# Gated linear attention with a gelu feed-forward: loads and weights no longer wait for each other, w_in in four pieces, and a new order of the instructions

## The chip, the core and the metric

The kernel runs on one core of a Trainium2 chip. The metric is the device time of one execution in microseconds (us), lower is better; the time before is the median of three runs. The core has five engines, each with a queue of its own that it works through in order: PE (matmuls; PEld is its weight load), DVE (vector), ACT (activation functions), POOL (GpSimd) and SP, which here only issues DMA transfers. POOL issues DMA transfers too. All transfers share 16 DMA engines.

## The reference

q, k, v and f_logit have the shape (4, 8, 768, 48): batch, heads, sequence, head dimension. Each head runs a gated linear recurrence over the sequence, and the result goes through a feed-forward layer with exact gelu.

```python
f = 1.0 / (1.0 + np.exp(-f_logit))
for t in range(S):
    state = f[:, :, t, :, None] * state + np.einsum('bhd,bhe->bhde', k[:, :, t], v[:, :, t])
    y[:, :, t] = np.einsum('bhd,bhde->bhe', q[:, :, t], state)
x = y.transpose(0, 2, 1, 3).reshape(B * S, H * D)     # 3072 x 384
h = x @ w_in                                          # 384 x 2048
g = 0.5 * h * (1.0 + erf(h * inv_sqrt2))
out = g @ w_out                                       # 2048 x 384
```

## The kernel before

The 3072 rows are 24 chunks of 128, numbered 0 to 23; two chunks make one of twelve units, numbered 0 to 11 (so "the second unit" is unit 1, "the third unit" unit 2). A unit is also one group of the feed-forward layer.

For each unit, f_logit, k, q and v (384 KB each) are loaded: names in the load list are a letter and the unit, so f0, k0, q0, v0. w_in comes in column pieces i0, i1, ..., w_out in four pieces o0 to o3; both are issued by POOL, and the data loads by SP.

The steps of a unit u with chunks n = 2u, 2u+1 are:

- E, L on ACT: exp and log of the gates. C on PE: their running sums (the C of unit 2 is C4). RG, GT, GL on ACT: exps of the sums. G on DVE: the second chunk's sum as a difference.
- KP, QP on DVE or POOL: k and q times these exps. VC on POOL or ACT: v cast to bf16.
- Tk, Tq on PE: transposes of both; KQ on DVE or ACT copies them out of PSUM. From unit 4 on a DMA transpose does this (KD).
- A on PE: scores. AM on DVE: mask. S on PE: state sum of a chunk pair. R on DVE, T and SB on POOL: the running state, and its cast to bf16.
- YI and YX on PE (or Y): output inside the pair, and from the state. YB on DVE or ACT: copy out. XT on PE and X on DVE or ACT: transposed into xT (later by a DMA transpose, XD).
- F1 on PE: eight steps of six matmuls for a group, each into one PSUM bank; GE on ACT: gelu of that bank, into gT. F2 on PE: for each chunk four steps of four matmuls; O copies out, and a store follows.

Step u of F1 reads w_in's columns 256u to 256u + 255, so with 1024 columns in the first piece steps 0 to 3 need i0 alone.

exp and log need another activation table than gelu. Wherever ACT goes from one to the other, a table load stands in its queue (ACT_TABLE_LOAD).

What sets the order is a list written out by hand: every step is added to a plan (`Plan.add`) with an engine and an assumed duration, and `ORDER` gives the sequence in which `Plan.run` places them. The placing gives each step a time from the assumed durations, waits and transfer times, and the instructions of each engine are then emitted by these times. The durations in the code thus decide order alone. While PE would idle in the first 30 us of the plan, it is given matmuls on a `junk` tile.

`load` adds the transfers in the sequence of `LOADS`. Where the sequence goes from SP's loads to POOL's weights or back, it looks backwards for a transfer of the other kind and makes the new one wait until that one has landed (`gate`).

Of the kernel before, what the change touches and what calls it, by code (L numbers as in the profile page):

```python
# [11 lines left out]
ALU = mybir.AluOpType  # L12
# [9 lines left out]
TURN = 0.1  # L22
# [53 lines left out]
class Plan:  # L76
# [30 lines left out]
    def run(self):  # L107
# [16 lines left out]
        while ready:  # L124
# [69 lines left out]
WIN = [1024, 512, 512]  # L194
# [8 lines left out]
HX = [0, 3, 9]  # L203
# [16 lines left out]
AHEAD = 4.4  # L220
UNITS = 12
WARM = 30.0
LOADS = ['f0', 'f1', 'k0', 'q0', 'v0', 'q1', 'k1', 'i0', 'v1', 'f2', 'q2', 'v2', 'k2', 'i1', 'i2', 'o0', 'o1', 'o3', 'o2', 'f3', 'f4', 'k3', 'q3', 'v4', 'v3', 'q4', 'k4', 'k5', 'f5', 'v5', 'q5', 'f6', 'v6', 'k6', 'q7', 'q6', 'f7', 'k7', 'v7', 'f8', 'k8', 'v8', 'q8', 'u9', 'u10', 'u11']
# [38 lines left out]
def kernel(  # L262
# [143 lines left out]

    def load(eng, issue, wr, bufs, dur, name):
        i = len(order)
        gate = None
        if i and eng != "act" and order[i - 1][0] != eng:  # L410
            ahead = 0.0
            late = None
            for j in range(i - 1, -1, -1):
# [3 lines left out]
                if order[j][0] != eng:  # L417
                    late = order[j][1]
# [285 lines left out]
    def compact(n):  # L704
        return rc[n] // nC in DENSE
# [576 lines left out]
```

## Time and profile before

| what | value |
|---|---|
| median of 3 runs (lowest, highest) | 179.34 us (178.78, 179.63) |
| profiled execution, first to last instruction | 178.1 us |
| PE busy | 168.7 us |
| ACT busy | 130.0 us |
| ACT table loads | 1 ahead of the first exp, and 17 |
| filler matmuls on PE (junk) | 26 |
| granted PE clock | 1.0 throughout |

The profiled execution is given on the page by its span, from its first instruction to its last. Rows of the timeline have start, duration, engine, line, operation, output and inputs, how many instructions are merged, and in brackets how long the engine was idle before and what ended that. Rows of stretches give the stretch and its length, then busy time and instruction count of PE, PEld, DVE, ACT and POOL, then the clock, the DMA share and GB/s. Rows of the chain have start, duration and what the time is put down to; SPq is SP's queue. Matmuls overlap by their fill and drain, so the chain's rows, which count from start to start, are better for adding up.

### The profile page before, as it was taken

The page shows a single profiled execution, that of the slowest core. Times are in us where ns is not written, and L with a number is a line of the kernel's source. Part 1 is how long each engine was busy: PE and PEld are TensorE (multiplying, and loading weights), DVE is VectorE, ACT ScalarE, POOL GpSimd, SP SyncE. Part 2 cuts the span into 40 slices and gives each one's busy share as a digit, 9 for nine tenths or more (in the row PEclk, how much of TensorE's full clock was granted, in tenths as well). Part 3 has the DMA queues.
Part 4 walks back from the last instruction along what each step waited for, and adds up shares of the span by engine and source line. Part 5 has one row for each costly group of instructions (what it writes and reads, how often), then busy time and mean ns, then how long its engine had stood idle before and what let it go on. Part 6 is the DMA issues. An engine that isn't in the chain of part 4 may idle for free.

```text
span 178.1 us, 4916 instructions
## 1 busy us (share of the span) xinstructions
PE 168.7 (95%) x1996; PEld 131.2 (74%) x1996; DVE 93.7 (53%) x188; ACT 130.0 (73%) x221; POOL 55.2 (31%) x119
## 2 busy tenths in 40 slices
PE   7787889999997999999999999999999999999993
PEld 2345679866787787886688689866797976887972
DVE  5188750067988556338677681246582276560110
ACT  2954399967797999989477597786684789951630
POOL 7267595041126801501052334002222504410000
PEclk9999999999999999999999999999999999999999
DMA  5999999999979898988999999999899975405412
GB/s 140 261 261 214 277 179 195 213 221 256 235 154 227 187 212 188 202 178 169 233 174 248 188 174 204 188 220 156 191 238 179 232 165 81 85 4 112 138 60 88
DMA packets 106997, 32.61 MB, mean 183 GB/s; under 512 B 102112, under 2 KB 106080, under 8 KB 106976
## 3 DMA queue, kind: packets, MB, share of 16 engines
q1 hardware_dynamic: 105056, 29.07, 79.0%
q0 software_dynamic: 1776, 3.15, 10.0%
q8 instruction: 15, 0.25, 0.6%
q10 hardware_dynamic: 144, 0.10, 0.2%
q14 instruction: 6, 0.05, 0.1%
HBM read 25.17 MB, written 4.72 MB: 168 GB/s over the span
## 4 chain that ended last, share of the span: by engine, by line
PE 72%; DMA 14%; SPq 6%; POOL 3%; issue 1%; DVE 1%; ACT 0%; DVEq 0%; POOLq 0%
PE ps L1165 30%; PE ps L1186 29%; DMA vt<-in_v_dram 6%; SPq L513 4%; DMA kt<-in_k_dram 4%; DMA kq<-sc 3%; PE ps L995 2%; PE ps L1031 2%; PE ps L1211 1%; DMA out_dram<-osb 1%; PE ps L585 1%; PE ps L969 1%; SPq L949 1%; SPq L1200 1%; POOL vb L647 1%
## 5 line engine op out<-in xcount | busy, mean ns | idle before, releaser
L1175 ACT ACTIVATE gT<-ps 128x512 bf16<-128x512 f32 x96 | 57.2, 665 | 18.4 <-PE ps L1165 17.6
L1165 PE MATMUL ps<-xT,win 128*128 128x256 bf16 x576 | 69.0, 273 | 0.8 <-DMA win<-in_moe_w_in_dram 0.7
L1186 PE MATMUL ps<-wout,gT 128*128 128x384 bf16 x368 | 67.0, 326 | 0.0
L1165 PEld LDWEIGHTS <-win 128*128 128x128 bf16 x576 | 61.7, 114 | 3.7 <-DMA win<-in_moe_w_in_dram 0.9
L1186 PEld LDWEIGHTS <-gT 128*128 128x128 bf16 x368 | 34.1, 98 | 18.7
L901 DVE TENSOR_TENSOR am<-ps,mask 128x512 bf16<-128x512 f32 x28 | 17.5, 683 | 18.5 <-PE ps L995 18.5
L1248 ACT ACT_TABLE_LOAD x17 | 21.8, 1283 | 0.3
L640 DVE TENSOR_TENSOR sc<-kt,rg 128x384 bf16<-128x384 f32 x19 | 11.5, 606 | 15.8 <-ACT rg L607 11.1
L1191 DVE COPY osb<-ps 128x384 f32<-128x384 f32 x20 | 10.7, 552 | 16.8 <-PE ps L1186 15.7
L927 POOL TENSOR_TENSOR tn<-rr,gl 128x384 f32<-128x384 f32 x12 | 10.7, 889 | 25.1 <-DVE rr L925 19.1
L647 POOL CAST vb<-vt 128x384 bf16<-128x384 f32 x18 | 9.5, 539 | 26.8 <-DMA vt<-in_v_dram 26.6
L901 DVE TENSOR_TENSOR am<-ps,maskp 128x512 bf16<-128x512 f32 x20 | 12.7, 683 | 5.3 <-PE ps L1061 3.8
L945 DVE CAST yb<-ps 128x384 bf16<-128x384 f32 x21 | 11.4, 555 | 7.6 <-PE ps L1031 5.6
L640 DVE TENSOR_TENSOR sc<-qt,gt 128x384 bf16<-128x384 f32 x20 | 13.3, 684 | 3.4 <-ACT gt L613 2.7
L558 ACT ACTIVATE fl<-fl 128x768 f32<-128x768 f32 x12 | 10.1, 842 | 5.0 <-DMA fl<-in_f_logit_dram 5.0
L932 POOL CAST sb<-tn 48x192 bf16<-48x192 f32 x30 | 10.7, 362 | 8.3 <-DVE tn L921 7.1
L613 ACT ACTIVATE gt<-ps 128x384 f32<-128x384 f32 x21 | 10.3, 495 | 3.8 <-PE ps L587 2.9
L607 ACT ACTIVATE rg<-ps 128x384 f32<-128x384 f32 x21 | 10.1, 494 | 3.5 <-PE ps L587 2.9
L640 POOL TENSOR_TENSOR sc<-kt,rg 128x384 bf16<-128x384 f32 x5 | 5.3, 1065 | 22.5 <-ACT rg L607 14.3
L561 ACT ACTIVATE lf<-fl 128x768 bf16<-128x768 f32 x12 | 10.2, 849 | 0.3
L925 DVE TENSOR_TENSOR rr<-ps,tn 128x384 f32<-128x384 f32 x12 | 6.7, 555 | 5.9 <-PE ps L1018 4.8
L1241 PE MATMUL ps<-junk 128*128 128x512 bf16 (+3 forms) x26 | 8.3, 448 | 1.3 <-POOL junk L1233 1.3
(85 smaller groups left out, 145.1 us busy)
## 6 DMA issues: line engine op xcount, KB each, us to landing
out_dram<-osb SPq DMA_DIRECT2D x19, 192.0 KB, 2.8
kt<-in_k_dram SPq DMA_DIRECT2D x14, 192.0 KB, 4.5
fl<-in_f_logit_dram SPq DMA_DIRECT2D x14, 192.0 KB, 3.9
vt<-in_v_dram SPq DMA_DIRECT2D x14, 192.0 KB, 3.9
qt<-in_q_dram SPq DMA_DIRECT2D x14, 192.0 KB, 3.7
fl<-in_f_logit_dram SPq DMA_DIRECT2D x5, 384.0 KB, 4.9
kt<-in_k_dram SPq DMA_DIRECT2D x5, 384.0 KB, 6.2
qt<-in_q_dram SPq DMA_DIRECT2D x5, 384.0 KB, 6.3
```

The lines of the kernel that those rows point to most:

```text
L613: P.add("ACT", 0.40, lambda g=gps[j], gtv=gtv: nc.scalar.activation(gtv(), g.t()[:, 0:HD].rearrange("q (p h d) -> q p h d", h=2, d=D), AF. ...
L640: P.add("POOL" if pl else "DVE", 0.80 if pl else 0.475, lambda a=a, y=y, j=j, w=w, pl=pl, b=(gtv if w else rg): (nc.gpsimd if pl else nc.v ...
L647: P.add("ACT" if hv else "POOL", 0.40 if hv else 0.47, lambda y=y, j=j, hv=hv: (nc.scalar.copy if hv else nc.gpsimd.tensor_copy)(y["vb"].t ...
L901: P.add("POOL" if pl else "DVE", 1.15 if pl else 0.61, lambda hh=hh, pl=pl: (nc.gpsimd if pl else nc.vector).tensor_tensor(ams[hh].t(), ap ...
L927: P.add("POOL", 0.83, lambda: nc.gpsimd.tensor_tensor(tn.t(), rr.t(), glb(), ALU.mult), rd=[("rr", n), ("gl", n)], wr=[("tn", n)], bufs=[r ...
L932: P.add("POOL", 0.36, lambda hh=hh: nc.gpsimd.tensor_copy(sb.t()[64 * hh:64 * hh + D, :, D * hh:D * hh + D], tn.t()[64 * hh:64 * hh + D, : ...
L945: P.add("ACT" if help_ else "DVE", 0.40 if help_ else 0.475, lambda: copier(help_)(yb.t()[:, i, :], yp.t()[:, 0:HD]), rd=[("yp", n)], wr=[ ...
L1165: nc.tensor.matmul(hps.t()[:, i * tok:(i + 1) * tok].rearrange("a (s t) -> a s t", s=s), col(fo)[:, kk, :], xT.t()[:, :, kk, :], start=(kk ...
L1175: nc.scalar.activation(to, fr, AF.Gelu)
L1186: nc.tensor.matmul(op.t()[:, 0:d_model], gT.t()[:, fo, s_ * C:(s_ + 1) * C], wout[fo // 4][:, fo % 4, :], start=(fo == 0), stop=(fo == FO ...
L1191: P.add("DVE" if od else "ACT", 0.475 if od else 0.40, lambda op=op, osb=osb, od=od: copier(not od)(osb.t(), op.t()[:, 0:d_model]), rd=[(" ...
L1248: nc.scalar.preload_act_table_set({"exp": "natural_log_exp_and_others", "gelu": "gelu_and_others"}[o.table])
```

## The change

The loads of SP wait for no weights any more, and the weights wait for loads at two points: i0 until unit 0's values (vt0) have landed, o1 until unit 2's keys (kt2) have. v1 goes ahead of w_in in the load list. w_in comes in four pieces of 512 columns in place of one of 1024 and two of 512. The second chunk's copies change engines: VC2 goes from POOL to ACT, T2 and the first half of SB2 from POOL to DVE, X3 from ACT to DVE. All assumed durations are changed, and with them the order.

```diff
-WIN = [1024, 512, 512]
+WIN = [512, 512, 512, 512]
-HX = [0, 3, 9]
+HX = [0, 9]
-AHEAD = 4.4
+VCE = {2: 'ACT'}
+FM = []
+TE = {2: 'DVE'}
+SBE = {(2, 0): 'DVE'}
+SBD = {"POOL": 0.38, "DVE": 0.22, "ACT": 0.27}
+GATE = {'i0': 'vt0', 'o1': 'kt2'}
-LOADS = ['f0', 'f1', 'k0', 'q0', 'v0', 'q1', 'k1', 'i0', 'v1', 'f2', 'q2', 'v2', 'k2', 'i1', 'i2', 'o0', 'o1', 'o3', 'o2', 'f3', ...]
+LOADS = ['f0', 'f1', 'k0', 'q0', 'v0', 'q1', 'k1', 'v1', 'i0', 'i1', 'i2', 'i3', 'f2', 'o0', 'k2', 'q2', 'v2', 'o1', 'o3', 'o2', 'f3', ...]
...
-                d += TABLE
+                t = max(t, free["ACT"] + TABLE)
...
     def load(eng, issue, wr, bufs, dur, name):
         i = len(order)
-        gate = None
-        if i and eng != "act" and order[i - 1][0] != eng:
-            ahead = 0.0
-            late = None
-            for j in range(i - 1, -1, -1):
-                if order[j][0] != eng and ahead >= (AHEAD if eng == "pool" else 1.4):
-                    gate = late if late is not None and ahead > 5.3 and eng == "pool" else order[j][1]
-                    break
-                if order[j][0] != eng:
-                    late = order[j][1]
-                ahead += order[j][1].dur
+        gate = dict((nm, x) for _, x, nm in order).get(GATE.get(name))
...
+    def copy_on(eng):
+        return {"ACT": nc.scalar.copy, "POOL": nc.gpsimd.tensor_copy, "DVE": nc.vector.tensor_copy}[eng]
...
-            hv = u in HVC
+            hv = VCE.get(n, "ACT" if u in HVC else "POOL")
...
-            P.add("POOL", 0.45, lambda: nc.gpsimd.tensor_tensor(small(tn), small(rr), glb(), ALU.mult),
+            e = TE.get(n, "POOL")
+            P.add(e, 0.29 if e == "DVE" else 0.54, lambda e=e: (nc.vector if e == "DVE" else nc.gpsimd).tensor_tensor(small(tn), small(rr), glb(), ALU.mult),
```

The order list itself is replaced. What it does is shown at three places, each before and after; tile numbers differ by one or two between the programs.

POOL at the start, before: win is w_in's piece, vb a cast of v, sc the products KP and QP of unit 1, sb the state cast SB0 that YX1 reads.

```order
L525 DMA win_70<-in_moe_w_in_dram 128x3x1024 [waits DMAHW3_49]
L647 CAST vb_103<-vt_85 128x384 [waits DMAHW4_49]
L647 CAST vb_104<-vt_85 128x384
L640 TENSOR_TENSOR sc_97<-qt_82,gt_115 128x8x48 [waits DMAHW5_49,Activation_49]
L640 TENSOR_TENSOR sc_98<-qt_82,gt_114 128x8x48 [waits Activation_49]
L640 TENSOR_TENSOR sc_97<-kt_78,rg_118 128x8x48 [waits DMAHW6_49]
L726 CAST sb_148<-tn_141 48x4x48 [waits DVE_49,Pool_49]
```

The first weight transfer is issued when unit 0's q has landed, and no other stands ahead of the state cast. The same place after the change:

```order
L519 DMA win_70<-in_moe_w_in_dram 128x3x512 [waits DMAHW4_49]
L644 CAST vb_104<-vt_86 128x384
L644 CAST vb_105<-vt_86 128x384
L637 TENSOR_TENSOR sc_98<-qt_83,gt_116 128x8x48 [waits DMAHW5_49,Activation_49]
L519 DMA win_71<-in_moe_w_in_dram 128x3x512
L637 TENSOR_TENSOR sc_98<-kt_79,rg_119 128x8x48 [waits DMAHW6_49]
L637 TENSOR_TENSOR sc_99<-qt_83,gt_114 128x8x48 [waits Activation_49]
L519 DMA win_72<-in_moe_w_in_dram 128x3x512
L724 CAST sb_149<-tn_142 48x4x48 [waits DVE_49]
L724 CAST sb_149<-tn_142 48x4x48 [waits Pool_49]
L644 CAST vb_107<-vt_87 128x384 [waits DMAHW7_49,Pool_49]
L519 DMA win_73<-in_moe_w_in_dram 128x3x512
```

The first piece waits for unit 0's v, the second and third are issued between the products, ahead of the state cast, and the fourth behind it and a cast of unit 1's v.

ACT behind the first copy into xT, before: fl and lf are E2 and L2 of unit 2, gT a gelu.

```order
L964 COPY xT_163<-ps_174 128x384
L558 ACTIVATE fl_91<-fl_91 128x768
L561 ACTIVATE lf_94<-fl_91 128x16x48
L1248 ACT_TABLE_LOAD
L1175 ACTIVATE gT_167<-ps_174 128x4x2x64
```

The exp and log of unit 2 stand ahead of the first gelu. After the change ACT has the table load and fourteen gelus behind the copy, and the last of these are followed by:

```order
L1177 ACTIVATE gT_169<-ps_174 128x4x2x64
L1177 ACTIVATE gT_169<-ps_172 128x4x2x64
L1250 ACT_TABLE_LOAD
L555 ACTIVATE fl_92<-fl_92 128x768
L558 ACTIVATE lf_95<-fl_92 128x16x48
L604 ACTIVATE rg_117<-ps_177 128x384
```

E2 and L2 have moved behind fourteen of the sixteen gelus of the first two groups, with a table load of their own.

SP from the last loads of unit 2 on, before: fl_89 and fl_90 are the gates of units 3 and 4, and DMASW is the semaphore of a weight transfer.

```order
L513 DMA vt_87<-in_v_dram 128x8x96 [waits DMAHW2_49]
L513 DMA kt_79<-in_k_dram 128x8x96 [waits DMAHW3_49]
L513 DMA fl_89<-in_f_logit_dram 128x8x96 [waits DMAHW4_49,DMASW5_49,Activation_49]
L513 DMA fl_90<-in_f_logit_dram 128x8x96 [waits DMAHW5_49,Activation_49]
```

The gates of unit 3 wait for a piece of w_out. The same place after the change:

```order
L507 DMA qt_84<-in_q_dram 128x8x96 [waits DMAHW2_49]
L507 DMA vt_88<-in_v_dram 128x8x96 [waits DMAHW3_49]
L507 DMA fl_90<-in_f_logit_dram 128x8x96 [waits DMAHW4_49,Activation_49]
L507 DMA fl_91<-in_f_logit_dram 128x8x96 [waits DMAHW5_49,Activation_49]
```

The wait for the weights is gone, and unit 2's keys now come ahead of its q and v.

More of the change, by code (lines that the diff above doesn't have):

```diff
@@ L429, in load @@
         prev = order[-1][1] if order else None
-        if prev is not None and eng != "act" and order[-1][0] != eng:
-            prev.lat = 2.2
         gd = [gate] if gate is not None else []
@@ L449, in load @@
             o.fn = lambda o=o: fn(o)
-        if 7 <= i and o.lat < 1.8:
-            o.lat = 2.0 if name == "i0" else 1.8 if i < 30 else 1.7
-        order.append((eng, o))
+        if eng != "act":
+            o.lat = LANDS.get(name, 1.36 if i < 7 else 1.55 if i < 13 else 1.65 if i < 22 else 2.5 if i < 27 else 3.3 if i < 45 else 2.4)
+        order.append((eng, o, name))
     def src(a, n):
@@ L645, in decays @@
                     port=True, name=f"{nm.upper()}{n}")
-            hv = u in HVC
-            P.add("ACT" if hv else "POOL", 0.40 if hv else 0.47, lambda y=y, j=j, hv=hv: (nc.scalar.copy if hv else nc.gpsimd.tensor_copy)(
+            hv = VCE.get(n, "ACT" if u in HVC else "POOL")
+            P.add(hv, {"ACT": 0.40, "POOL": 0.47, "DVE": 0.3}[hv], lambda y=y, j=j, hv=hv: copy_on(hv)(
                 y["vb"].t().rearrange("p (h d) -> p h d", h=H), half(u, x["vt"], j)),
@@ L725, in carry_hs @@
             for hh, r in enumerate(rows):
-                P.add("POOL", 0.30, lambda hh=hh, r=r: nc.gpsimd.tensor_copy(sb.t()[r, :, D * hh:D * hh + D], small(tn)[r]),
+                e = SBE.get((n, hh), "POOL")
+                P.add(e, SBD[e], lambda hh=hh, r=r, e=e: copy_on(e)(sb.t()[r, :, D * hh:D * hh + D], small(tn)[r]),
                       rd=[("tn", n)] + z_sb, wr=[("sb", n, hh)], bufs=[tn, sb], prio=pr + 2, name=f"SB{n}")
@@ L900, in mask_scores @@
                 continue
-            P.add("POOL" if pl else "DVE", 1.15 if pl else 0.61, lambda hh=hh, pl=pl: (nc.gpsimd if pl else nc.vector).tensor_tensor(
+            P.add("POOL" if pl else "DVE", 1.15 if pl else 0.605, lambda hh=hh, pl=pl: (nc.gpsimd if pl else nc.vector).tensor_tensor(
                 ams[hh].t(), aps[hh].t().rearrange("p (h t) -> p h t", t=C),
@@ L931, in carry @@
         for hh in range(2):
-            P.add("POOL", 0.36, lambda hh=hh: nc.gpsimd.tensor_copy(
+            P.add("POOL", 0.38, lambda hh=hh: nc.gpsimd.tensor_copy(
                 sb.t()[64 * hh:64 * hh + D, :, D * hh:D * hh + D],
@@ L1065, in attn_pair @@
                 if jk:
-                    P.add("PE", 0.70, lambda: [b[1]() for b in both], mode=1, rd=[("kq", n) for n in ns],
+                    P.add("PE", 0.485, lambda: [b[1]() for b in both], mode=1, rd=[("kq", n) for n in ns],
                           wr=[("ap", u, 0), ("ap", u, 1)], bufs=[kq] + sum([b[2] + b[3] for b in both], []),
@@ L1175, in gelu @@
                 nc.scalar.activation(to, fr, AF.Gelu)
-            P.add("ACT", 0.60 if perm(ns[0]) and ns[0] // 2 not in RST else 0.50, gelu, rd=[("h", g, u)], wr=[("gT", g, u)], bufs=[hps, gT], table="gelu", prio=pr - 1000,
+            P.add("ACT", 0.585 if perm(ns[0]) and ns[0] // 2 not in RST else 0.49, gelu, rd=[("h", g, u)], wr=[("gT", g, u)], bufs=[hps, gT], table="gelu", prio=pr - 1000,
                   name=f"GE{'q' * (s == 4)}{g}.{u}")
```

46 lines of the change are left out of this document (25 added, 21 removed), and 62 rows, old and new, of the table ORDER.

## The prediction

> **What bounds the kernel now.** I read the page's totals first, then busy time by stretch, then the chain that ended last, then the start engine by engine.
>
> ```profile
> span 178.1 us, 4916 instructions
> PE 168.7 (95%) x1996; PEld 131.2 (74%) x1996; DVE 93.7 (53%) x188; ACT 130.0 (73%) x221; POOL 55.2 (31%) x119
> ```
>
> PE (the matmuls) is busy for 95% of the span. The stretches say where the rest is:
>
> ```profile
> 0.00:19.30 19.30, 14.48 (x216) 7.96 (x216) 11.54 (x40) 10.74 (x19) 10.76 (x33) 1.00 1.08 226
> 19.30:25.00 5.70, 5.20 (x110) 4.12 (x111) 3.78 (x8) 3.78 (x5) 5.03 (x11) 1.00 1.14 233
> 24.92:173.00 148.08, 146.99 (x1651) 117.40 (x1649) 77.89 (x140) 115.26 (x197) 39.52 (x76) 1.00 0.89 179
> ```
>
> From 24.92 on PE is idle for only 148.08 - 146.99 = 1.09 us. Its work is the same after the change, so it can gain in two ways only: reach the unbroken part sooner, and lose those 1.09 us. Nearly all of them are one wait:
>
> ```profile
> 54.35 0.52 PE L1093 MATMUL ps<-vb,sc 64*128 64x96 bf16 x16 [0.94 <-POOL vb L647]
> 52.51 1.01 POOL L640 TENSOR_TENSOR sc<-kt,rg 128x384 bf16<-128x384 f32 x1 [3.79 <-DMA kt<-in_k_dram]
> 53.46 0.83 POOL L647 CAST vb<-vt 128x384 bf16<-128x384 f32 x1
> ```
>
> S3, the state sum of the fourth unit, waits 0.94 us for a cast of its values, which stands on POOL behind a product for unit 4 that waited 3.79 us for its keys.
>
> PE's steps, for counting, are rows of the chain:
>
> ```profile
> 28.46 5.24 PE ps L1165 x48
> 33.70 4.55 PE ps L1186 x28
> 67.20 0.51 PE ps L1113 x32
> 57.80 0.28 PE ps L975 x4
> 59.38 0.34 PE ps L961 x6
> ```
>
> An F1 step (6 matmuls) is 6 x 5.24 / 48 = 0.655 us, an F2 step (4 matmuls) 4 x 4.55 / 28 = 0.65 us; the last three are the attention pieces YI, YX and XT.
>
> **The change, part 1: when F1 can start.** The first F1 step needs xT of unit 0 and the first piece of w_in:
>
> ```profile
> 9.45 0.94 POOL L525 DMA_DIRECT2D win<-in_moe_w_in_dram  x1 [3.90 <-DMA qt<-in_q_dram]
> 10.72 0.95 POOL L647 CAST vb<-vt 128x384 bf16<-128x384 f32 x2 [0.33 <-DMA vt<-in_v_dram]
> 12.31 1.00 POOL L640 TENSOR_TENSOR sc<-qt,gt 128x384 bf16<-128x384 f32 x1 [0.64 <-ACT gt L613]
> 14.58 1.31 POOL L640 TENSOR_TENSOR sc<-kt,rg 128x384 bf16<-128x384 f32 x1
> 15.96 0.74 POOL L726 CAST sb<-tn 48x192 bf16<-48x192 f32 x2
> 21.36 0.81 POOL L525 DMA_DIRECT2D win<-in_moe_w_in_dram  x1
> 16.89 0.34 PE L975 MATMUL ps<-sb,kq 128*128 128x96 bf16 x4
> 18.34 0.36 DVE L964 COPY xT<-ps 128x384 bf16<-128x384 bf16 x1 [0.79 <-PE ps L961]
> 19.35 1.50 PE L1165 MATMUL ps<-xT,win 128*128 128x256 bf16 x12 [0.69 <-DMA win<-in_moe_w_in_dram]
> ```
>
> Before, xT was there at 18.70 (18.34 + 0.36) and w_in's 1024 columns half a microsecond later. The order rows show that POOL now issues i0 after the values of unit 0 have landed (10.65, just before the cast), so the casts behind it start 0.9 later, and that i1 and i2 stand ahead of SB0, the state cast that YX1 waits for. POOL's list from 10.65: 0.94 + 0.95 + 1.00 + 0.81 + 1.31 + 1.00 + 0.81 + 0.74 = 8.56, which would end at 19.2 if nothing overlapped; instructions on POOL start some 0.05 before the one ahead ends, the product lasts 1.00 without a neighbour on DVE, and the first of those issues (0.94) is nearer to 0.81: 7.4 to 8.56. I take 7.4, since the rows that follow one another closely are the shorter ones, so SB0 ends at 18.05 where it ended at 16.70. From there to the end of the xT copies the rows give 18.70 - 16.70 = 2.0: xT at 20.05, F1 at **20.1**, 0.8 later than now; 21.3 at the other end. Of the moved small operations, VC2 goes to ACT, which waits there for PE anyway; T2, half of SB2 and X3 go to DVE. I cost these at nothing; uncovered, each is the 0.3 to 0.5 us of its row.
>
> **Part 2: gelu ahead of the third unit's exp.** Now ACT does E2 and L2 and a table load between the first F1 steps and their gelus:
>
> ```profile
> 20.97 0.84 ACT L558 ACTIVATE fl<-fl 128x768 f32<-128x768 f32 x1 [2.32 <-DMA fl<-in_f_logit_dram]
> 21.85 0.84 ACT L561 ACTIVATE lf<-fl 128x768 bf16<-128x768 f32 x1
> 22.71 1.28 ACT L1248 ACT_TABLE_LOAD   x1
> 24.00 0.76 ACT L1175 ACTIVATE gT<-ps 128x512 bf16<-128x512 f32 x1
> ```
>
> The first gelu is at 24.00, and until then PE has room for three F1 steps only. In the order rows the table load follows the xT copy, so gelus can start at about 21.4 and PE runs on from 20.1: five F1 steps (3.27) with YI1, two YX and the XTs (0.51 + 0.56 + 0.34) end at 24.8. The sixth step reads the fourth piece of w_in. POOL issues that after SB0 and one cast (0.48), at 18.5:
>
> ```profile
> DMA to landing us min/median/max: 6.4/6.6/9.9
> ```
>
> This row is of w_in: 6.4 to 6.6 for the 512-column pieces, 9.9 for the 1024-column one. Landing is 18.5 + 6.5 = **25.0**, so PE waits 0.2; at the other end it is 18.5 + 9.9 = 28.4. I take 25.0, by the rows of the same size.
>
> Then comes the price of the new place of E2. Fourteen gelus stand ahead of it. The fourteenth is that of F1 step 14, which ends at 25.0 + 9 x 0.655 = 30.9. Gelu 0.76, table 1.28, E2 and L2 21.85 + 0.84 - 20.97 = 1.72: C4, the decay sums of unit 2, can start at **34.7**. PE has two F1 and two F2 steps in between and stands at C4 at 33.5: a wait of 1.2 us that is not there now. After C4 follow one F2 step and Tk4, which waits for KP4:
>
> ```profile
> 23.92 0.16 PE ps L590
> 24.08 0.16 PE ps L591
> 24.24 0.18 PE ps L579 x8
> 36.27 0.52 ACT L607 ACTIVATE rg<-g 128x384 f32<-128x384 f32 x1
> 37.25 1.00 POOL L640 TENSOR_TENSOR sc<-kt,rg 128x384 bf16<-128x384 f32 x1 [8.05 <-ACT rg L607]
> ```
>
> C4 takes 0.5 (to 35.2), the exp 0.52, KP4 on POOL 1.00: Tk4 at **36.85**, where PE has arrived at 35.85, so it waits another 1.0.
>
> Now the comparison at equal work. At Tk4 PE has done all of units 0 and 1, C4, 16 F1 and 3 F2 steps. Before, it had at 24.92 done the same but 13 F1 and 3 F2 steps, and it ran on without a wait apart from 0.11 of filler: 24.92 + 13 x 0.655 + 3 x 0.65 + 0.11 = 35.5. **After is 1.35 us behind there.** Afterwards both have the same left.
>
> **Part 3: loads that wait for no weights.**
>
> ```profile
> SPq L513 <- DMA wout<-in_moe_w_out_dram: 15.1, 1, 15.1
> 8.82 10.76 DMA vt<-in_v_dram
> 45.31 7.07 DMA kt<-in_k_dram
> ```
>
> SP stood 15.1 us until w_out was in; the order rows no longer have that semaphore. The values of unit 1 took 10.76 us beside i0 and now go ahead of it. Unit 3's loads can only come sooner, and POOL has unit 3's casts ahead of KP8, so the wait of 0.94 at S3 goes: **-0.94**. What is late next there is A3, far behind. The one new wait for loads is o1 behind the keys of unit 2; mask, two casts, T3 and KP4 are queued behind it on POOL. It costs nothing if those keys are in by about 31, which leaves 0.6 + 0.2 + 1.5 and the other issues before KP4 at 35.75; each microsecond beyond is one at Tk4.
>
> **Part 4: more switches.** ACT has 5 more table loads in the whole program than now:
>
> ```profile
> L1248 ACT ACT_TABLE_LOAD x17 | 21.8, 1283 | 0.3
> ```
>
> Each is 1.28 of ACT; ACT was idle for 48 us and PE has F2 steps beside them: 0, with 1.28 apiece where none is left. In the rows above the gelu starts at 24.00, right where the load of 22.71 ends. By the Trainium skill, "ScalarE: Activation LUTs", What ACT_TABLE_LOAD costs, a switch takes about 2.66 us, since a drain of 1.38 comes to the 1.28. By that C4 would come 1.4 later and the time would be some 181; the rows have no such drain, and the measurement decides.
>
> **Sum.** 178.1 + 1.35 - 0.94 = 178.5 of span. The page gives the profiled execution by its span; the median of 179.34 lies 1.24 above it, and I add that: **179.8**, a quarter of a per cent over the time before. About 0.5%, or 0.9 us, is what a measurement can tell from no change.
>
> **Rivals.**
>
> *The start gains (faster).* POOL's list is shorter than I think, F1 starts at 19.4 as before, and the fourth piece is there when PE comes: Tk4 is 0.95 sooner, and the last gelu takes 0.1 less than the first. Then after is only 0.3 behind, and with -0.94 and the other 0.15 of idle time it is 0.8 faster: 178.5. For it: each POOL figure has slack. Against: the wait at C4 comes from ACT's own list and no early weight removes it.
>
> *Weights and loads hold each other up (slower).* Loads now flow while w_in does:
>
> ```profile
> q1 hardware_dynamic: 2765, 1.04, 128.3%
> q0 software_dynamic: 356, 0.73, 89.1%
> q1 hardware_dynamic: 484, 0.19, 23.6%
> ```
>
> The first row is 5.0 to 9.0, loads alone: 691 packets per us. The others are 13.2 to 17.5, i0 beside them: the loads fall to 113 per us, about as many as the weights' 83. With 512 columns a weight packet is half as large, so at a packet for a packet the pieces get a smaller part. Then the fourth lands between 25.0 and 28.4, say 27.0, and everything behind it is 2.0 later: 181.8. It decides from 25.5 on, and the casts for unit 2, whose values come last, would hold KP4 as well. The Trainium skill, "DMA: Bandwidth & Descriptors", Queues, rings and completion order, states that each DMA engine goes round its queues packet by packet, and the two counts agree with that roughly.
>
> *A table load without cover (slower).* One of the five surfaces at PE: 181.1; two: 182.4.
>
> **How the numbers follow.** Forecast 0.45, start gains 0.25, shared DMA 0.21, table load 0.09. The first rival stands at the edge of 0.5%, and what its stages add on either side I count 0.21 beyond; with a little of the forecast on each side: faster 0.22, within 0.5% 0.45, slower 0.33. The range goes from a little under the first rival to the second and most of the third: 178.2 to 182.0.
>
> **What would show it.** Right: the first F1 at about 20.1, then PE without filler; a wait of about 1.2 before the C of unit 2 put down to ACT's lf, about 1.0 before its first transpose put down to POOL; none before S3. Wrong: F1 before 19.5; a wait of PE on win over 0.6; no wait at C4; waits of over 0.5 behind 55 us; a landing of unit 2's keys behind 31.

## The result, and the profile after

| | before | after |
|---|---|---|
| median of 4 runs (lowest, highest) | 179.49 us (178.78, 179.88) | 187.25 us (186.81, 188.34) |
| ratio, 95% interval | | 1.0459 [1.0426, 1.0493] |
| profiled execution, and its span | 178.1 (span) | 186.81, span 185.0 |

The change makes the kernel 4.6% slower. The prediction of 179.8 (178.2 to 182.0) missed by 7.45 us: 6.5 of that is the span (178.5 predicted, 185.0 measured), and 1.0 is what lies around it (1.24 taken from the median of before, 187.25 - 185.0 = 2.25 after). Some executions of a kernel come out slower than its others; the ratios leave these out and the medians do not, so the two can differ a little below.

These are the totals of the page after, and the clock in forty slices:

```profile
span 185.0 us, 4898 instructions
PE 171.6 (93%) x1990; PEld 132.0 (71%) x1991; DVE 92.3 (50%) x191; ACT 136.5 (74%) x226; POOL 55.1 (30%) x117
PEclk9999589999999999999999999999999999999999
```

PE does the same matmuls in a longer span, and one slice early on runs at half clock. The stretches that were shown of before:

```profile
0.00:19.30 19.30, 13.52 (x192) 7.46 (x193) 11.12 (x38) 10.69 (x19) 12.76 (x36) 0.97 1.11 227
19.30:25.00 5.70, 5.70 (x82) 3.95 (x76) 3.81 (x8) 2.61 (x4) 3.03 (x8) 0.52 1.20 217
24.92:173.00 148.08, 143.39 (x1654) 113.80 (x1653) 75.36 (x141) 121.69 (x201) 39.31 (x74) 1.00 0.89 176
```

From 19.30 to 25.00 PE looks full, but at a clock of 0.52: 82 matmuls where before had 110. And the unbroken part is broken: idle time from 24.92 on is 148.08 - 143.39 = 4.69 us, where it was 1.09. PE's timeline names the waits:

```profile
18.41 0.48 PE L977 MATMUL ps<-sb,kq 128*128 128x96 bf16 x4 [1.11 <-POOL sb L724]
21.14 3.90 PE L1167 MATMUL ps<-xT,win 128*128 128x256 bf16 x18
...
28.22 6.75 PE L1167 MATMUL ps<-xT,win 128*128 128x256 bf16 x60 [0.57 <-DMA win<-in_moe_w_in_dram]
...
38.17 0.32 PE L587 MATMUL ps<-lf,trip 128*128 128x384 bf16 x1 [1.25 <-ACT lf L558]
...
40.49 0.40 PE L878 MATMUL ps<-ident,sc 128*128 128x128 bf16 x4 [0.98 <-POOL sc L637]
41.19 0.40 PE L878 MATMUL ps<-ident,sc 128*128 128x128 bf16 x4 [0.30 <-DVE sc L637]
...
43.47 1.47 PE L1188 MATMUL ps<-wout,gT 128*128 128x384 bf16 x8 [0.32 <-ACT gT L1177]
...
55.46 0.51 PE L1095 MATMUL ps<-vb,sc 64*128 64x96 bf16 x16
...
145.74 0.82 PE L1167 MATMUL ps<-xT,win 128*128 128x256 bf16 x6 [0.67 <-DMA xT<-yb]
```

Read from the top: YX1 waits for the state cast; F1 starts at 21.14, three steps taking 3.90 us where they would take 3 x 0.655; the first step on the fourth piece of w_in starts at 28.22; C4 waits 1.25 for the log of unit 2, Tk4 0.98 for KP4; S3 at 55.46 waits for nothing. The waits of C4 and Tk4 are the predicted ones, to 0.05 us.

Waits alone miss time at half clock and time for which PE had work of another place to do. So I also count **lost time at equal work**: the start of a matmul minus the work that PE has done before it, each matmul counted with the median from its start to the next one's in the trace of before, filler as nothing. By this count, in us:

```
work done      20      26      90     148
before      12.57   12.65   12.74   12.86
after       15.01   18.84   18.08   20.06
after-before +2.44   +6.19   +5.34   +7.20
```

Work 20 is reached at 35.1 after, 26 (behind Tk4) at 44.9, 90 at 108.2. So 2.4 go in the start, 3.8 around C4 and Tk4, 0.9 come back by S3, and another 1.9 go behind 105 us.

### The profile page after: what moved, and what is told of

It is laid out like the page before. It is cut to its first block, busy times and chain, and to the rows that moved or that the text cites. A ratio compares the mean times of both kernels' runs of the same rounds, so it can differ in the third digit from the quotient of the medians.

```text
span 185.0 us, 4898 instructions
## 1 busy us (share of the span) xinstructions
PE 171.6 (93%) x1990; PEld 132.0 (71%) x1991; DVE 92.3 (50%) x191; ACT 136.5 (74%) x226; POOL 55.1 (30%) x117
## 4 chain that ended last, share of the span: by engine, by line
PE 61%; DMA 16%; ACT 10%; POOL 4%; SPq 3%; DVE 2%; issue 2%; DVEq 0%
PE ps L1167 26%; PE ps L1188 23%; DMA win<-in_moe_w_in_dram 5%; ACT gT L1177 5%; DMA vt<-in_v_dram 3%; DMA xT<-yb 3%; DMA kq<-sc 3%; ACT L1250 2%; SPq L507 2%; POOL sc L637 2%; PE ps L997 2%; DMA out_dram<-osb 2%; PE ps L1213 1%; PE ps L1033 1%; DVE yb L947 1%
## 5 line engine op out<-in xcount | busy, mean ns | idle before, releaser
L1177 ACT ACTIVATE gT<-ps 128x512 bf16<-128x512 f32 x96 | 58.0, 664 | 24.2 <-PE ps L1167 23.7
L1167 PE MATMUL ps<-xT,win 128*128 128x256 bf16 x576 | 71.7, 277 | 1.6 <-DMA xT<-yb 0.9
L1188 PE MATMUL ps<-wout,gT 128*128 128x384 bf16 x368 | 68.8, 326 | 0.3 <-ACT gT L1177 0.3
L1167 PEld LDWEIGHTS <-win 128*128 128x128 bf16 x576 | 62.7, 115 | 6.9 <-issue 1.8
L1188 PEld LDWEIGHTS <-gT 128*128 128x128 bf16 x368 | 33.5, 97 | 18.3 <-ACT gT L1177 0.7
L637 DVE TENSOR_TENSOR sc<-kt,rg 128x384 bf16<-128x384 f32 x19 | 12.4, 657 | 10.9 <-ACT rg L604 10.9
L644 POOL CAST vb<-vt 128x384 bf16<-128x384 f32 x17 | 8.7, 524 | 29.6 <-DMA vt<-in_v_dram 29.6
L637 DVE TENSOR_TENSOR sc<-qt,gt 128x384 bf16<-128x384 f32 x20 | 11.5, 578 | 2.1 <-ACT gt L610 1.3
L878 PE MATMUL ps<-ident,sc 128*128 128x128 bf16 x64 | 5.9, 220 | 2.7 <-POOL sc L637 2.0
L1243 PE MATMUL ps<-junk 128*128 128x512 bf16 (+2 forms) x20 | 6.6, 456 | 1.4 <-POOL junk L1235 1.3
```

The costliest lines, as they stand in the source:

```text
L637: P.add("POOL" if pl else "DVE", 0.92 if pl else 0.475, lambda a=a, y=y, j=j, w=w, pl=pl, b=(gtv if w else rg): (nc.gpsimd if pl else nc.v ...
L1167: nc.tensor.matmul(hps.t()[:, i * tok:(i + 1) * tok].rearrange("a (s t) -> a s t", s=s), col(fo)[:, kk, :], xT.t()[:, :, kk, :], start=(kk ...
L1177: nc.scalar.activation(to, fr, AF.Gelu)
L1188: nc.tensor.matmul(op.t()[:, 0:d_model], gT.t()[:, fo, s_ * C:(s_ + 1) * C], wout[fo // 4][:, fo % 4, :], start=(fo == 0), stop=(fo == FO ...
```

## The experiments

Eighteen kernels in five sets. Steps are moved by a list that takes a step out of the placed order and emits it right ahead of another; below only the list is shown (where the cast ahead of KP8 is tried by itself, it works on the order list before the placing):

```diff
+    for nm, ahead in MOVE:
+        at = lambda x: next(i for i, o in enumerate(P.placed) if o.name == x)
+        o = P.placed.pop(at(nm))
+        P.placed.insert(at(ahead), o)
```

### Is it the half clock, or the late piece?

**After, with seven filler matmuls ahead of Tq3 and YX1.**

```diff
+FILL = {'Tq3': (2, 'A1.1'), 'YX1': (5, 'A1.1')}
```

> The changed kernel with seven more filler matmuls of 512 columns on PE, two ahead of Tq3 and five ahead of YX1, where PE stood idle from 16.2 to 18.4. Theory (two delays lie one over the other: the half clock of 18.0 to 24.8, and the fourth piece of w_in that lands only at 28.2): the clock is 1.0 in all forty slices, the work from 18.4 to 27.4 takes 2.9 us less, and PE waits that much longer for the same piece, about 3.5 us in place of 0.7: 187.0, between 186.5 and 187.5. Rival (the half clock is itself what makes the kernel slow): 2.9 us less, 184.3. If the filler does not keep the clock up, nothing changes: 187.2.

**After, with unit 2's loads held until the fourth piece of w_in is in.** fl2 is the load of unit 2's gates.

```diff
-GATE = {'i0': 'vt0', 'o1': 'kt2'}
+GATE = {'i0': 'vt0', 'o1': 'kt2', 'fl2': 'i3'}
```

> The changed kernel with one wait more: the loads from unit 2's f_logit on wait on SP until the fourth piece of w_in is in. Theory (loads and weights share the DMA engines packet by packet, and that is why the piece issued at 18.9 lands at 28.2): the fourth piece lands before 25, PE's wait of 0.7 for it at 27.4 is gone, the half clock stays since it is set before: 186.3, between 185.8 and 186.8. Rival (the landing is set by POOL's issues and the four pieces run one behind the other anyway): it lands at 27 or later and the time stays at 187.2. Second rival (unit 2's loads are then too late for E2 or for the casts): a new wait at C4 or Tk4 and over 187.5.

**Both together.**

> Both edits of the two runs before. Theory (each delay hides the other, so only both together pay): about 3.3 us less than the changed kernel, 184.0, between 183.3 and 184.8, far more than the two alone together. Rival (they add up): the sum of what the two runs alone give, about 186.

Measured: 187.18, 187.26 and 187.48 us (ratios 1.0412 [1.0352, 1.0472], 1.0415 [1.0343, 1.0487], 1.0429 [1.037, 1.0489]); none differs clearly from after's 1.0459. Two stretches after (the one ahead of the slow clock, and the slow one), then the first of them with filler:

```profile
14.60:18.00 3.40, 2.06 (x46) 1.20 (x45) 2.53 (x6) 1.52 (x2) 3.35 (x4) 0.99 1.21 225
18.00:24.75 6.75, 6.34 (x92) 4.58 (x91) 4.10 (x10) 2.99 (x4) 4.15 (x10) 0.50 1.20 221
```

```profile
14.60:18.00 3.40, 3.19 (x53) 1.66 (x51) 2.52 (x5) 1.52 (x2) 3.40 (x4) 1.00 1.21 225
```

With filler PE's timeline has, at the fourth piece, the first row below; the second is the page's clock in forty slices:

```profile
28.31 1.94 PE L1167 MATMUL ps<-xT,win 128*128 128x256 bf16 x16 [1.53 <-DMA win<-in_moe_w_in_dram]
PEclk9999999988999999999999999999999999999999
```

With PE kept busy the clock stays at 1.0 in the start, and the time that this saves is spent waiting for w_in: lost time at work 20, reached at 35, is 15.1 in both. **The half clock of the start costs nothing by then; it lies beside the wait for the fourth piece.** The clock is not full to the end with filler: it is 0.50 from 40.1 to 43.5, so the times of 187.18 and 187.25 alone would not show it. Holding the loads back brings w_in in 2.5 us sooner (last packet at 25.20 for 27.69 in the packet records) and the start gains 2.75 at work 20. Then F2 of unit 0 waits for w_out, which the other gate keeps behind unit 2's late keys:

```profile
38.90 1.44 PE L1188 MATMUL ps<-wout,gT 128*128 128x384 bf16 x4 [2.81 <-DMA wout<-in_moe_w_out_dram]
```

The clock also goes to 0.51 behind that wait, from 37.7 to 44.5. So sharing the DMA engines with the loads does cost w_in 2.5 us, but the loads are then missing. My theory, that only both edits together pay, fell: the gate alone gains 2.75 of the 3.0 that both gain in the start, and the third kernel loses it at the same w_out, with the clock at 0.50 from 36.3 to 43.1.

**After, with that load gate in place of o1's.**

```diff
-GATE = {'i0': 'vt0', 'o1': 'kt2'}
+GATE = {'i0': 'vt0', 'fl2': 'i3'}
```

> The changed kernel with the loads from unit 2's f_logit on waiting for the fourth piece of w_in, as in e2_gate, but without the wait of o1 for unit 2's keys. Theory (in e2_gate and e3_filler_gate the start gained 2.8 us at equal work, and all of it went into the new wait for the second piece of w_out, 2.2 to 2.8 us): no wait for w_out, Tk4 some 2.5 us sooner than in the changed kernel, 184.9, between 184.3 and 185.6. Rival (unit 2's values land behind 37 then, and the casts hold KP4 at the same place): Tk4 again at 40 and 187.

192.26 us, 1.0714 [1.0649, 1.0779]: neither expectation. Weights now go ahead of unit 2's gates, and PE's timeline shows what is late:

```profile
38.67 0.48 PE L587 MATMUL ps<-lf,trip 128*128 128x384 bf16 x1 [5.33 <-ACT lf L558]
44.42 1.04 PE L878 MATMUL ps<-ident,sc 128*128 128x128 bf16 x8 [3.46 <-POOL sc L637]
```

### What the cast ahead of KP8 is worth by itself

**Before, with unit 3's cast VC6 ahead of KP8 on POOL.**

```diff
+MOVE = [('VC6', 'KP8')]
```

> The kernel before, with one step moved: VC6, the cast of unit 3's values that S3 waits for, goes on POOL ahead of KP8, the product for unit 4 that waited 3.8 us for its keys. Theory (the wait of S3 is that position and nothing else): the wait of 0.94 before S3 is gone and nothing takes its place, 178.6, between 178.3 and 178.9. Rival (another step of unit 3 or 4 is late next, such as KP8 itself): 179.3 to 179.6.

Median of 12 runs 178.94 against 179.40, ratio 0.9978 [0.995, 1.0006]. PE's timeline of this kernel at S3, with no wait now:

```profile
53.14 0.51 PE L1097 MATMUL ps<-vb,sc 64*128 64x96 bf16 x16
```

The wait of 0.94 is gone; lost time at work 148 falls by 1.3 in the profile, the median by 0.46, and the interval reaches just past no change. The theory had 178.3 to 178.9. The profile falls by more because the profiled execution of before was some 0.85 slower than its median (the base, below).

### The place of E2

**After, with unit 2's exp and log (and their load in the order) ahead of the first gelu, and C4 ahead of the F1 step that reads the fourth piece.**

```diff
+MOVE = [('fl2', 'GE0.3'), ('E2', 'GE0.3'), ('L2', 'GE0.3'), ('C4', 'F1.0.6')]
```

> The changed kernel with E2 and L2 ahead of the first gelu on ACT, and C4 on PE ahead of the F1 step that waits for the fourth piece. Theory (two delays lie one over the other at Tk4 too: KP4 comes after RG4 on ACT, but also behind VC5, VC4 and T3 on POOL, which wait for values that land at 37.4): the wait of 1.4 before C4 is gone and nearly all of it comes back before Tk4, which starts at 40.0 in place of 40.5: 186.7, between 186.3 and 187.2. Rival (the place of E2 is the only cause there): both waits go, 184.8.

**The opposite, in before: E2, L2, C4 and G5 behind the gelus of the first two groups.**

```diff
+MOVE = [('E2', 'RG5'), ('L2', 'RG5'), ('C4', 'RG5'), ('G5', 'RG5')]
```

> The kernel before with E2 and L2 of unit 2 behind the sixteen gelus of units 0 and 1, and C4 and G5 behind them, where the change has put them. Theory (this place alone costs about 3 us, since e6_e2_early took them away and gained 3.1): 3 us more than before, between 181.5 and 182.7, with a new wait of PE before C4 put down to ACT. Rival (the place costs only where loads and weights come late as well): 0.5 us more or less.

After with E2 early: 184.14 us, 1.0298 [1.0223, 1.0373], 3.1 us below after (2.9 by the ratios); my theory of 186.7, that POOL's casts hold Tk4, fell. Before with E2 late: 183.25 against 179.87, 1.0191 [1.0145, 1.0237], 3.4 above before in the median. Undone in one kernel and done in the other, **moving E2 is worth about 3 us**, the largest gain of any single step. The 3.4 is more than after's own place would cost, since E2 stands there behind all sixteen gelus, two more than in after. ACT's timeline of after with E2 early, then PE's of before with E2 late:

```profile
20.02 0.84 ACT L555 ACTIVATE fl<-fl 128x768 f32<-128x768 f32 x1 [0.59 <-DMA fl<-in_f_logit_dram]
20.89 0.84 ACT L558 ACTIVATE lf<-fl 128x768 bf16<-128x768 f32 x1
21.76 1.28 ACT L1254 ACT_TABLE_LOAD   x1
23.05 2.17 ACT L1177 ACTIVATE gT<-ps 128x512 bf16<-128x512 f32 x3
```

```profile
38.15 0.32 PE L590 MATMUL ps<-lf,trip 128*128 128x384 bf16 x1 [2.40 <-ACT lf L561]
```

In the first, exp and log fit into time in which ACT has no gelu to do anyway, C4 follows at 26.18 without a wait, and the first gelu is at 23.05, sooner than after's 23.93 although it now has E2 and L2 ahead. In the second, C4 waits 2.40 for the log, with the pieces of w_in and the loads issued as in before.

Lost time says where the 3.1 lies: 1.05 in the start (15.01 to 13.96 at work 20) and 1.93 between work 20 and 26 (3.83 to 1.90), where E2 stood. The part in the start is not ACT's: C4's work of some 0.5 now fills PE's wait for the fourth piece, and in this execution that piece was also issued 0.54 sooner (at 18.33 for 18.87), with the clock at 1.0.

**E2 early, and the casts VC4, VC5 and the product T3 behind KP4 on POOL.**

```diff
 MOVE = [('fl2', 'GE0.3'), ('E2', 'GE0.3'), ('L2', 'GE0.3'), ('C4', 'F1.0.6'),
+        ('VC5', 'SB3'), ('VC4', 'SB3'), ('T3', 'SB3')]
```

> As e6_e2_early, and on POOL KP4 ahead of VC5, VC4 and T3. Theory (both at once): RG4 at 36.4, KP4 done at 37.9, Tk4 at 38.0, 2.5 us sooner than in the changed kernel: 184.9, between 184.2 and 185.5. Rival (S2 then waits for the casts, and the gain is given back within 2 us): 186.5.

183.66 us, 1.0235 [1.0178, 1.0292]. Lost time between work 20 and 26 is 1.9 with and without this, so POOL's casts were not what holds Tk4; the two intervals overlap, so the difference of 0.5 to the kernel with E2 early is not told from none.

### What w_in in four pieces costs once E2 is early

**E2 early, and unit 2's keys behind the fourth piece.**

```diff
-GATE = {'i0': 'vt0', 'o1': 'kt2'}
+GATE = {'i0': 'vt0', 'o1': 'kt2', 'kt2': 'i3'}
```

> e6_e2_early with unit 2's keys, and so every load behind them on SP, waiting for the fourth piece of w_in. Theory (what is left of the start, 1.4 us at equal work, is w_in sharing the DMA engines with unit 2's loads): the waits of F1 for w_in, 2.3 us in e6_e2_early, go nearly all; keys and values still land ahead of KP4 at 36: 182.4, between 181.8 and 183.0. Rival (o1 waits for those keys, and comes too late for the F2 steps, as in e2_gate): 184 or more.

**E2 early, with the three pieces of before.**

```diff
-WIN = [512, 512, 512, 512]
+WIN = [1024, 512, 512]
```

> e6_e2_early with w_in in three pieces again, 1024, 512 and 512 columns. Theory (with 1024 columns a packet is twice as large and gets twice the bytes beside the loads; one issue less stands on POOL): the first piece lands 0.6 later and the last 1.5 to 2 sooner, the waits of F1 for w_in fall from 2.3 to about 1: 183.0, between 182.4 and 183.5. Rival (the bytes come at the same rate in either form): 184.1.

**The same, with the third piece's issue behind SB0.**

```diff
+        ('ii2', 'VC3')]
```

> e11_three_pieces with the third weight transfer issued behind SB0 on POOL. Theory (the issues ahead of the state cast delay YX1, as the prediction had it, by 0.75, and with three pieces nothing hides it): the wait of 1.1 before YX1 falls to 0.3, F1 starts 0.7 sooner: 183.0, between 182.6 and 183.3. Rival (F1 then waits for the first piece of w_in instead): 183.7.

184.28 us (1.0215 [1.0139, 1.0291]), 183.69 (1.0216 [1.0175, 1.0257]) and 184.66 (1.0226 [1.0169, 1.0282]). Of the gate only the time is used. With three pieces, no wait in PE's timeline is put down to w_in (the plan sees F1's first step late and runs filler ahead of it, to 21.70, then 21.26). YX1 waits for SB0, which moving the issue mends:

```profile
18.32 0.33 PE L978 MATMUL ps<-sb,kq 128*128 128x96 bf16 x4 [1.11 <-POOL sb L725]
```

```profile
17.67 0.33 PE L978 MATMUL ps<-sb,kq 128*128 128x96 bf16 x4 [0.29 <-POOL sb L725]
```

The start is 0.5, then 0.9 better at work 20 (13.96, 13.49, 13.07), and the time, within what these intervals tell apart, the same as with E2 early alone, so theories and rivals are not told apart. Another order of the F1 steps, with the fourth piece asked for last, wasn't tried.

### What is lost behind 105 us

**After, with two DMA transposes of xT ahead of unit 9's loads on SP.**

```diff
+MOVE = [('XD13', 'fl9.0'), ('XD15', 'kt9.1')]
```

> The changed kernel with two DMA transposes sooner on SP: XD13 ahead of unit 9's loads, behind eight of whose issues it stood for 5.4 us (its input was there at 100.5, its issue at 105.9), and XD15 ahead of one load and one store. Theory (the waits of F1 at 109.3 to 112 are SP's queue): these 0.66 us go, the waits at 132 and 145 stay: 186.6, between 186.2 and 186.9. Rival (they come from something else, such as the copy out of the PSUM bank): no change, 187.2.

190.13 us, 1.0492 [1.0396, 1.0588]; my theory, that this order costs the 1.9, fell. PE waits for xT no longer, but the output of a chunk is late behind the transpose, and F1 waits for it by way of the bank in PSUM (DVE's and PE's timeline):

```profile
113.24 0.56 DVE L1193 COPY osb<-ps 128x384 f32<-128x384 f32 x1 [2.06 <-DMA out_dram<-osb]
```

```profile
113.85 1.36 PE L1167 MATMUL ps<-xT,win 128*128 128x256 bf16 x11 [1.80 <-DVE osb L1193]
```

**E2 early, and chunk 2's store ahead of chunk 3's.** In after that store is ready at 65.65 and issued at 163.46.

```diff
+        ('st2', 'st3')]
```

> e6_e2_early with one store moved on SP: that of chunk 2, which is ready at 65.7 in the changed kernel and issued at 163.5, goes ahead of the store of chunk 3. Theory (it holds one of the four output buffers for 98 us, so the copies out of PSUM at 109 to 112 wait for a buffer, and F1 for the bank): the waits of F1 put down to osb, 0.6 and 0.4, go: 183.2, between 182.8 and 183.6. Rival (the other stores that stand behind loads, 10 to 21 us late, hold the copies as well): no change, 184.1.

186.9 us (183.61 to 188.24), 1.0266 [1.0178, 1.0355]: the runs scatter too widely to tell. Unclear; nothing speaks for the theory.

**E2 early, with two stores and both transposes ahead of unit 9's loads.**

```diff
+        ('st6', 'fl9.0'), ('st8', 'fl9.0'), ('XD13', 'fl9.0'), ('XD15', 'kt9.1')]
```

> e6_e2_early with SP's list changed at one place: the stores of chunks 6 and 8 (ready at 94, issued at 104.7 and 108.3 in the changed kernel) and the transpose XD13 go ahead of unit 9's loads, XD15 ahead of the load that follows. Theory (F1's waits at 109 to 112 are for a PSUM bank whose copy has no output buffer, since two of the four are held by stores that stand behind six loads on SP; e8_sp_order pushed these stores further back and its wait for osb grew from 0.2 to 1.8): the waits for osb and xT between 105 and 115 fall from 1.0 in e6_e2_early to under 0.3: 183.2, between 182.8 and 183.6. Rival (the stores are not what holds the copies): 184.1.

**That, with three pieces, SB0 first and KP4 early.**

> The repairs of e6, e7, e11, e13 and e14 in one kernel. Theory (each acts at a place of its own, so they add up): from 183.7 of e11_three_pieces take 0.9 for the stores, 0.7 for SB0 and 0.5 for KP4: 181.6, between 181.0 and 182.2, still 2 us over the kernel before, and that rest is the two gelus and the table load that stand behind unit 2's exps. Rival (they hide each other as the start and w_out did in e3 and e9): 183 or more.

186.33 us (1.0384 [1.035, 1.0418]) and 186.05 (1.035 [1.0299, 1.0402]): neither faster than E2 early alone (1.0298), though the second has every repair in it. The waits for osb and xT are gone, and now the gates of a later unit are late, so exp, gelu and F1 are (ACT's and PE's timeline of the first):

```profile
108.50 0.85 ACT L555 ACTIVATE fl<-fl 128x768 f32<-128x768 f32 x1 [3.45 <-DMA fl<-in_f_logit_dram]
```

```profile
112.18 3.08 PE L1167 MATMUL ps<-xT,win 128*128 128x256 bf16 x26 [2.75 <-ACT gT L1177]
```

**Stores of chunks 0 to 15 issued by POOL: in E2 early, in after, and in before with VC6 ahead of KP8.**

```diff
-                    nc.sync.dma_start(out=out[...], in_=osb.t()[r:r + w, :])
+                    (nc.gpsimd if n < 16 else nc.sync).dma_start(out=out[...], in_=osb.t()[r:r + w, :])
```

> e6_e2_early with the stores of chunks 0 to 15 issued by POOL in place of SP, at the same places of the order. Theory (SP is full: 9.0 to 9.6 of every 10 us between 60 and 140 are its issues, so an entry that is put forward there puts another back, which is why e8 and e13 only moved the wait to osb and to the gelus; POOL is 30% busy): SP has some 0.6 us less to issue for each store, the waits of F1 between 105 and 145 go, 1.4 us less than e6_e2_early: 182.7, between 182.2 and 183.2. Rival (the stores' place in the order is too late on any queue, or POOL's casts now come late behind them): 184 or more.

> The changed kernel with the same edit alone. Theory: the 1.9 us that it loses between 105 and 150 fall to under 0.5: 185.7, between 185.1 and 186.3. Rival: 187.2 or more.

> e4_before_cast with the same edit. Theory (SP is as full there, but its transposes and loads are not late for PE, which stands nowhere behind 55 us, so nothing is to be had): as e4_before_cast, within 0.4 us. Rival (SP's slack is worth something there too, at the end, where its queue runs out last): 0.5 us or more below it.

186.72 us (1.037 [1.0305, 1.0435]), 188.75 (1.0509 [1.046, 1.0558]) and 180.37 against 179.2 (1.0053 [1.0026, 1.0079]); each ratio lies above that of the same kernel with the stores on SP. The first two came out as their rivals had it, though the intervals overlap; in the last, which neither expectation had, they are apart. In after the loss behind work 90 falls from 1.98 to 0.44, in E2 early it stays (1.4 for 1.5). And a store from POOL lands late, so that ACT waits for its buffer (ACT's and PE's timeline of the second):

```profile
79.95 0.48 ACT L1193 COPY osb<-ps 128x384 f32<-128x384 f32 x1 [1.69 <-DMA out_dram<-osb]
```

```profile
80.48 1.69 PE L1167 MATMUL ps<-xT,win 128*128 128x256 bf16 x14 [1.55 <-ACT osb L1193]
```

In it lost time rises by 1.18 from work 26 to 90, where it falls by 0.76 in after, and by 2.2 more than in after from 20 to 26; beside this its clock is 0.50 from 40.3 to 47.1, where after's is 1.00, so the 2.2 cannot be put down to the stores.

## Why the prediction was wrong, step by step

**The base of 178.1 + 1.24: 0.85 off.** Executions of before with both numbers on record lie 2.1 over their span (179.37 with 177.2, 180.19 with 178.1), those of after 1.8. So the profiled execution of before was one of some 180.2 us, by these numbers, and the median belongs to a span nearer 177.2. The spans differ by 6.9, the medians by 7.76.

**F1 can start at 20.1: off by 1.0, and not what counts.** The terms of POOL's list add up to 7.56, not to 8.56, so the other end was 18.2 for SB0 and 20.3 for F1, not 21.3; after took 7.51 from 10.84. SB0 ended at 18.35 (17.59 + 0.76) for 18.05, F1 began at 21.14, since YX and the XTs ran at half clock, which no step of the prediction foresaw; that this is close to 21.3 is chance. With the clock at 1.0 F1 began at 20.32 with filler and at 19.79 with E2 early. The filler showed that this costs nothing by work 20.

**Gelus from about 21.4: right, to 0.3.** ACT's table load ran from 20.42 to 21.70. The first gelu came at 23.93 because its F1 step did.

**The fourth piece lands at 25.0: the step that failed first.** It was priced by the rows of 512-column pieces before (6.4 to 6.6); the chain after has

```profile
18.87 9.30 DMA win<-in_moe_w_in_dram
```

and the tile view of win, over all pieces,

```profile
DMA to landing us min/median/max: 8.1/8.6/9.3
```

The landing is 28.17, 3.2 later than taken and near the other end (28.4) that I had kept and not chosen. The rows of before were of other conditions: the first 512-column piece was issued at 21.36 with nothing ahead in its queue (the packets of the piece ahead ended at 18.88), the second at 23.49 with one piece ahead, and from 24 to 28 only 74 packets of loads moved, against 1264 after. After, the packet records show the four pieces one behind the other (14.56 to 18.39, 18.29 to 21.45, 21.36 to 24.10, 24.01 to 27.69), so the fourth, issued at 18.87, stood 5.1 us behind its elders before its first packet moved. This is rival 2 in its mechanism, at a higher price: it forecast 27.0, decided from 25.5 on. Holding back unit 2's loads showed 2.5 us of it to be sharing with them. What the lateness costs in the end stays open: the gate got 2.75 back in the start and lost it at w_out, and with E2 early and three pieces no wait for w_in is left, but lost time at work 26 is only 0.5 lower (15.86 to 15.38). All of w_in is in sooner than before (27.7 for 29.35); but before runs eight F1 steps on the first piece, while after's order wants the third and fourth piece at its fifth and sixth step.

**Fourteen gelus ahead of E2 cost 1.2 at C4 and 1.0 at Tk4: right, to 1.25 and 0.98.** C4 came at 38.17 for 34.7, which is the 3.2 of the fourth piece and a quarter of a microsecond in the gelus. Tk4 came at 40.49 for 36.85. At equal work after was there not 1.35 but about 5.0 behind, 3.2 of the 3.6 between them by the fourth piece. Moving E2 got 1.93 back between work 20 and 26, where the sum had 2.2. The waits of 0.30 at Tk5 and 0.32 at F2 behind it are not E2's, since they are the same with E2 early (PE's timeline of that kernel):

```profile
37.51 0.40 PE L878 MATMUL ps<-ident,sc 128*128 128x128 bf16 x4 [0.46 <-POOL sc L637]
38.21 0.40 PE L878 MATMUL ps<-ident,sc 128*128 128x128 bf16 x4 [0.30 <-DVE sc L637]
40.48 1.48 PE L1188 MATMUL ps<-wout,gT 128*128 128x384 bf16 x8 [0.32 <-ACT gT L1177]
```

No term of the sum had these two, nor the short gaps around them: after loses about another 1.2 from Tk4 (5.0) to work 26 (6.2).

**S3's 0.94: the mechanism right.** The wait is gone, lost time falls by 0.85 between work 26 and 90. As a change by itself it showed 0.46 in the median, so the profiled execution of before may have had a longer wait than most.

**Loads that wait for no weights cost nothing: the gate was right, the cover was not.** o1's gate opened at 25.8, well ahead of 31; the price is in the previous points, since the loads took their share from w_in.

**Table loads at nothing: right.** The page's row of them, after:

```profile
L1250 ACT ACT_TABLE_LOAD x22 | 28.2, 1283 | 1.1 <-PEq L1268 0.7
```

These are 5 more, at 1.28 each, and PE shows one wait of 0.32 behind one (43.47), so rival 3, which needed 1.28 at PE, fell. By the Trainium skill, "ScalarE: Activation LUTs", What ACT_TABLE_LOAD costs, each switch would take 2.66 us; the gelu at 23.05 with E2 early starts 1.29 after its load does, so the trace disagrees.

**"Afterwards both have the same left": the other step that failed**, by 1.9 behind 105 us. It left SP's queue out. Its rows, added up from its timeline, fill 8.7 to 9.5 of every 10 us from 60 to 140 in both kernels; in 50 to 60 before had 9.4 and after 4.3, since SP stood waiting. But a row is not only issuing: from 20 to 40 after, six issues fill 9.8 of 10 us too, two of which take 12.07 us together, so these shares are an upper bound, and the expectations above that call SP full took them for more. SP's timeline after, where YB's casts for a pair of chunks are done at 100.5:

```profile
100.41 0.63 SPq L515 DMA_DIRECT2D fl<-in_f_logit_dram  x1
101.09 0.92 SPq L515 DMA_DIRECT2D kt<-in_k_dram  x1
...
104.66 1.15 SPq L1202 DMA_DIRECT2D out_dram<-osb  x1
105.91 1.72 SPq L951 DMA_TRANSPOSE xT<-yb  x1
```

Their transpose is issued at 105.91, behind loads and a store, and F1 at 109.92 waits for it. The waits are so placed by the rows. That SP's full queue is the cause was argued and not shown: each transfer that was moved forward made another late, and taking the stores from SP cut the loss behind work 90 in one kernel and not in the other, and made neither faster.

**Rival 1, the start gains: fell.** The start lost 2.44.

The sum with what was measured: about +6.2 up to Tk4 and the steps behind it for +1.35, -0.85 for -0.94, +1.9 for 0, and -0.3 in the last steps, so that 6.9 of span came out for 0.4; the base makes it 7.76 in the medians.

Of the signs of being wrong one came, the wait of 0.67 at 145.74. PE's wait on win was 0.57, under the 0.6 of its sign, though the piece was 3.2 late: PE was late itself, and a late transfer shows in PE's waits only by what PE has not lost already.

What stays open: of the 5.3 us that the kernel with E2 early is still slower than before, 1.4 lie in the start by its lost time, 1.8 between work 20 and 26 and 1.4 behind 90. The middle part shows waits of 0.46, 0.30 and 0.32 at Tk4, Tk5 and F2 in PE's timeline; the rest of it is short gaps between the transposes that no experiment here took apart. At Tk4 the exps for KP4 still stand behind the fourteen gelus and a table load there (the load at 34.59, the first exp at 35.88 in ACT's timeline).

## What to carry to other kernels

Price a transfer by what stands ahead of it in its own queue and by what else moves at that time, not by an earlier row of the same size; and check at which step of the consumer each piece is first asked for. When a step of another activation table is moved, look for the time in which that engine idles already (here ahead of the first gelu): outside of it, the steps behind it pay. "The rest is the same" has to be checked on the queue that issues transfers as well, since here each transfer moved forward made another late. And look whether the profiled execution is a typical one before building on its span.

## What the runs showed of the hardware

**The clock fell without a long pause.** PE was busy 2.06 of 3.40 us ahead of 18.0, with no pause over the 1.11 ahead of YX1, and then had 0.50 for 6.75 us. With the loads held back it was busy hardly more in the same stretch, with E2 early less, and the clock stayed there in both:

```profile
14.60:18.00 3.40, 2.18 (x47) 1.25 (x46) 2.53 (x6) 1.52 (x2) 3.40 (x4) 1.00 1.19 190
```

```profile
14.60:18.00 3.40, 1.90 (x50) 1.33 (x48) 3.15 (x5) 1.52 (x2) 3.28 (x6) 1.00 1.19 232
```

The Trainium skill, "TensorE: Matmul & The Clock Gate", Part 1, tells of a free-running window of 3.4 us and a half rate after an idle one; two such windows are about the 6.75, but no window here was idle, so the trace shows that a partly busy one can do. The clock fell at 2.06 and stayed at 1.90 and 2.18, so the busy share of this stretch does not decide it, and these runs give no threshold.

**Loads and weights do not share packet for packet.** From 14.6 to 18.8 after, the two kinds of queue moved (packets, MB, share):

```profile
q0 software_dynamic: 471, 0.47, 65.6%
q1 hardware_dynamic: 1274, 0.48, 54.0%
```

1 to 2.7 in packets and about 1 to 1 in bytes, where the prediction's second rival took it from 83 and 113 per us before that they take turns; from 19 to 24 it was 689 to 1070. The Trainium skill, "DMA: Bandwidth & Descriptors", Queues, rings and completion order, has turns by packet, a packet being typically 9 to 17 descriptors. A packet of these counts is some 1000 bytes of w_in or 380 of a load, and no run shows how many of them make one turn, so the counts neither bear that out nor refute it.

**An issue is not free for its engine.** SP's plain issues last 0.57 to 1.15 us in its rows after from 99 to 112 us and a transpose 1.26 to 1.72, so some ten fill 10 us. A row takes in whatever the issue waits for inside it, so the shorter ones are nearer to the price.
